# Attention lanes by head parity instead of key parity, values in one phase, and x loaded first, in a fused sliding-window attention and gated MLP kernel

## The chip, the cores and the metric

The kernel runs on one core of one Trainium2 chip. The metric is the device time of one execution in microseconds, the median of several runs. The kernel before takes 281.9 us (three runs, 280.76 to 282.53).

An execution can fall into a slower state; such runs are marked slow.

A matrix multiply on TensorE shows in the traces as two instructions, a weight load (PEld) and the matmul proper (PE): 4336 of each on the page of the kernel before. I call the two a *pair*.

## The reference, cut to what matters

```python
# x: 1 x 2048 x 512, bf16; 32 heads of 16; window 256; F = 1792
xn  = layernorm(x)
q, k, v = split(xn @ wqkv)                       # per head 2048 x 16
s   = q @ k.T * 16**-0.5
s   = where((i - j >= 0) & (i - j < 256), s, -1e9)
att = softmax(s) @ v                             # back to 2048 x 512
out = x + att @ wo + ((xn @ w_gate) * (xn @ w_up)) @ w_down
```

## The kernel before: the parts that matter

The tokens are worked off in four chunks T of 512, and in each chunk there are four groups c of eight heads, so there are 16 (T, c) pairs of attention work. A chunk has eight blocks of 64 queries. A block of queries needs five blocks of keys: its own (masked by one triangle), the one four back (masked by the other triangle) and the three between (not masked). Scores lie as keys x queries in `S`; ACT exponentiates them to `P`; POOL zeroes the triangles with selects; the values matmul then multiplies `P` by `V`, with a column of ones that gives the softmax sum.

All of this has contractions of 16 (scores) or 64 (values), so the kernel cuts TensorE's array, which a dense matmul takes as a whole (128*128 in the page's shapes), into eight tiles for it: four tiles `e`, times two *lanes* of 64 rows or columns. The rest (projections, gate, up, down, output) is 128 x 128 x 512 "dense" work. A small list scheduler in the kernel orders the work before it is issued, and drops attention blocks into the run of dense matmuls.

Before, a lane holds the key blocks of one *key parity*. V is laid out with 128 tokens on the partitions, so that key block `j` is in lane `j % 2`. A head's output needs keys of both parities, which means that both lanes add into the same PSUM place; the kernel keeps these two additions apart in time, so the values come in two phases, with a drain and a semaphore between them:

```python
def i_values(self, T, c, strips, phase, banks, begun):
    if phase == 1:
        self.nc.tensor.wait_ge(self.turn, self.v)
    # ... todo: the segments (key block k, m query blocks from q) whose head parity is lane ^ phase
    for _, lane, par, k, q, m, at, P in sorted(todo, key=lambda t: t[:2]):
        U, j = divmod(8 * T + k, 8)
        for e in range(4):
            self.nc.tensor.matmul(
                banks[par][32 * e:32 * e + 17, 64 * q:64 * (q + m)],
                lhsT=self.V[U % 3][64 * lane:64 * lane + 64, j // 2, 8 * c + 2 * e + par, 0:17],
                rhs=P[64 * lane:64 * lane + 64, e, 64 * at:64 * (at + m)],
                start=(par, e) not in begun, stop=phase == 1, tile_position=(64 * lane, 32 * e), ...)
    if phase == 0:
        self.nc.tensor.drain().then_inc(self.turn, 1)
```

The scores go out in batches (five per pair, four in chunk 0), the V projection is four plain dense matmuls per 128 tokens, and the loads and a run of useless matmuls (the *warm-up*) stand at the top:

```python
load(nc.sync,   self.x[:, 0, :], ...);  load(nc.scalar, self.Wqkv[:, :, 1024:1536], ...)   # Wv
load(nc.sync,   self.x[:, 1, :], ...);  load(nc.scalar, self.Wqkv[:, :, 512:1024], ...)    # Wk
load(nc.sync,   self.x[:, 2, :], ...);  load(nc.sync, self.x[:, 3, :], ...)
load(nc.sync,   self.Wqkv[:, :, 0:512], ...)                                               # Wq
# ... gate, up, down, output weights, the rest of x
for _ in range(40):        # the warm-up: useless matmuls
    nc.tensor.matmul(self.M[0][:, 0:128], lhsT=self.ident[:], rhs=self.ident[:], start=True, stop=True)

def matmuls(self, ps, pairs, first=True, last=True):        # all dense work
    for n, (a, b) in enumerate(pairs):
        self.nc.tensor.matmul(ps, lhsT=a, rhs=b, start=first and n == 0, stop=last and n == len(pairs) - 1)
```

The softmax here doesn't subtract the row's maximum and nothing guards it: scores larger than these inputs give would overflow.

## Time and profile before

| | kernel before |
|---|---|
| median time | 281.9 us |
| span of the profiled run | 279.4 us |
| PE busy | 96% |
| score + value matmuls | 1664 + 1664 |
| first score block | 18.15 us |

PE is the bottleneck: busy for nearly the whole span and first in the chain. The instruction queue moved 34 packets, 0.56 MB.

The timeline of the kernel before, PE only, around one pair (start us, us, engine, line, operation, count), shows an attention block between dense work: values phase one, a score batch, values phase two.

```profile
180.32 0.59 PE L218 MATMUL M<-xnT,Wg 128*128 128x512 bf16 x2
180.85 0.74 PE L255 MATMUL M<-P,V 64*17 64x64 bf16 x56
181.73 0.42 PE L226 MATMUL S<-Q,K 16*64 16x320 bf16 x16
182.09 0.77 PE L255 MATMUL M<-P,V 64*17 64x128 bf16 x56
182.79 1.04 PE L218 MATMUL M<-xnT,Wu 128*128 128x512 bf16 x4
```

I cost a block from the starts: the time from the last dense start before it to the first after it, minus one dense step (0.216 us). So costed, a score batch takes 0.45 us, and values-scores-values 2.04 us. There are no waits inside. The same view at the start of the kernel shows the first score batch at 18.15 us, and the view of the waits (waiter <- what it waited for: us in total, times, longest) shows that the layernorm statistics wait for x:

```profile
18.15 0.42 PE L226 MATMUL S<-Q,K 16*64 16x320 bf16 x16
```

```profile
DVE st L267 <- DMA x<-in_A_x_dram: 2.8, 3, 1.5
```

### The profile page before, as it was taken

How to read it: one execution, taken by the hardware profiler on the slowest of the kernel's cores; microseconds unless marked ns; L12 is line 12 of the kernel's file. 1: busy time of each engine (PE TensorE's matmuls, PEld its weight loads, DVE VectorE, ACT ScalarE, POOL GpSimd, SP SyncE). 2: the span in 40 equal slices, each digit the busy share in tenths (PEclk: the TensorE clock that was granted, in tenths of full speed). 3: DMA queues.
4: the chain of work that ended last, by engine and by line, in shares of the span. 5: the costliest groups of instructions: out<-in, count | busy, mean ns of one | idle time of the engine just before them, and what ended most of it. 6: DMA issues, size and time to landing. Idle time of an engine off the chain costs nothing.

```text
span 279.4 us, 9843 instructions
## 1 busy us (share of the span) xinstructions
PE 266.8 (96%) x4336; PEld 122.7 (44%) x4336; DVE 183.9 (66%) x323; ACT 150.8 (54%) x91; POOL 210.9 (75%) x447
## 2 busy tenths in 40 slices
PE   6699999999999999999999999999999999999994
PEld 5354444444444444444444444444444444444441
DVE  4668986879893508677884539687781518687503
ACT  2125756756575666576574756554566666564000
POOL 3208898879799999988799897879499999879000
PEclk9799999999999999999999999999999999999999
DMA  7999240000005100000005300000000000000002
GB/s 224 371 372 348 81 77 2 2 2 2 2 0 79 39 21 25 0 6 0 5 0 72 64 22 2 2 2 2 2 4 21 21 21 21 1 5 0 5 0 75
DMA packets 17050, 14.00 MB, mean 50 GB/s; under 512 B 7024, under 2 KB 17008, under 8 KB 17008
## 3 DMA queue, kind: packets, MB, share of 16 engines
q1 hardware_dynamic: 15952, 12.32, 15.6%
q10 hardware_dynamic: 1056, 1.05, 1.2%
q8 instruction: 34, 0.56, 0.9%
q14 instruction: 8, 0.07, 0.1%
HBM read 9.70 MB, written 2.10 MB: 42 GB/s over the span
## 4 chain that ended last, share of the span: by engine, by line
PE 83%; POOL 9%; DMA 2%; DVE 2%; issue 2%; ACT 1%; SPq 0%; ACTq 0%
PE M L218 68%; PE S L226 9%; POOL P L236 8%; PE M L255 6%; DMA x<-in_A_x_dram 2%; ACT P L498 1%; POOL rs L273 0%; PE M L592 0%; SPq L168 0%; DVE xnT L214 0%; DVE st L267 0%; DVE hT L688 0%; DVE gsb L214 0%; DVE V L214 0%; DVE y L709 0%
## 5 line engine op out<-in xcount | busy, mean ns | idle before, releaser
L236 POOL TENSOR_SCALAR_AFFINE_SELECT P<-P 64x256 bf16<-64x256 bf16 (+1 forms) x424 | 202.9, 501 | 40.7 <-ACT P L498 31.5
L498 ACT ACTIVATE P<-S 128x2048 bf16<-128x2048 f32 x76 | 142.6, 1877 | 86.8 <-PE S L226 77.7
L218 PE MATMUL M<-xnT,Wu 128*128 128x512 bf16 x224 | 57.7, 380 | 0.1
L218 PE MATMUL M<-xnT,Wg 128*128 128x512 bf16 x224 | 57.7, 380 | 0.0
L218 PE MATMUL M<-Wd,hT 128*128 128x512 bf16 x224 | 54.5, 380 | 0.5
L688 DVE TENSOR_TENSOR hT<-M,gsb 128x512 bf16<-128x512 f32 x56 | 37.9, 677 | 10.6 <-PE M L218 10.2
L532 DVE STREAM_TRANSPOSE at<-M 128x512 f32<-128x512 f32 x32 | 21.2, 696 | 25.7 <-PE M L255 25.5
L214 DVE CAST gsb<-M 128x512 bf16<-128x512 f32 x46 | 31.5, 686 | 7.2 <-PE M L218 6.7
L709 DVE TENSOR_TENSOR y<-M,x 128x512 bf16<-128x512 f32 x16 | 11.0, 689 | 34.7 <-PE M L218 34.6
L218 PEld LDWEIGHTS <-Wu 128*128 128x128 bf16 x224 | 20.3, 98 | 24.7 <-issue 1.3
L218 PE MATMUL M<-xnT,Wqkv 128*128 128x512 bf16 (+1 forms) x152 | 31.0, 351 | 0.0
L218 PEld LDWEIGHTS <-Wg 128*128 128x128 bf16 x224 | 20.1, 98 | 24.4 <-issue 1.2
L218 PEld LDWEIGHTS <-hT 128*128 128x128 bf16 x224 | 19.8, 98 | 24.9 <-issue 2.8
L255 PE MATMUL M<-P,V 64*17 64x192 bf16 (+4 forms) x1664 | 23.6, 240 | 0.5 <-POOL P L236 0.5
L255 PEld LDWEIGHTS <-V 64*17 64x17 bf16 x1664 | 17.4, 85 | 12.6 <-issue 8.9
L218 PEld LDWEIGHTS <-Wqkv 128*128 128x128 bf16 x152 | 13.4, 101 | 14.3 <-issue 0.9
L226 PE MATMUL S<-Q,K 16*64 16x192 bf16 (+3 forms) x832 | 17.4, 248 | 1.2
L218 PE MATMUL M<-Wqkv,xnT 128*128 128x512 bf16 x64 | 16.5, 396 | 1.6 <-DVE xnT L214 0.9
L226 PE MATMUL S<-Q,Ko 32*64 32x128 bf16 (+3 forms) x832 | 17.1, 245 | 0.1
L218 PE MATMUL M<-Wo,OT 128*128 128x512 bf16 x64 | 16.8, 380 | 0.3
L226 PEld LDWEIGHTS <-K 16*64 16x64 bf16 x832 | 7.8, 103 | 17.7 <-issue 16.5
L226 PEld LDWEIGHTS <-Ko 32*64 32x64 bf16 x832 | 8.1, 104 | 13.4 <-issue 13.4
(38 smaller groups left out, 133.1 us busy)
## 6 DMA issues: line engine op xcount, KB each, us to landing
out_dram<-y SPq DMA_DIRECT2D x16, 128.0 KB, 1.7
Wg<-in_B_w_gate_dram SPq DMA_DIRECT2D x2, 896.0 KB, 10.1
Wu<-in_B_w_up_dram SPq DMA_DIRECT2D x2, 896.0 KB, 11.5
Wd<-in_B_w_down_dram SPq DMA_DIRECT2D x1, 1792.0 KB, 17.7
Wqkv<-in_A_wqkv_dram ACTq DMA_DIRECT2D x2, 512.0 KB, 5.4
x<-in_A_x_dram SPq DMA_DIRECT2D x1, 1024.0 KB, 14.2
x<-in_A_x_dram SPq DMA_DIRECT2D x4, 128.0 KB, 5.0
Wqkv<-in_A_wqkv_dram SPq DMA_DIRECT2D x1, 512.0 KB, 6.7
```

Source lines behind the costliest of these rows:

```text
L214: self.nc.vector.tensor_copy(out=out, in_=in_)
L218: self.nc.tensor.matmul(ps, lhsT=a, rhs=b, start=first and n == 0, stop=last and n == len(pairs) - 1)
L226: self.nc.tensor.matmul(self.S[64 * lane:64 * lane + 64, e, 64 * at:64 * (at + m)], lhsT=(self.Ko if par else self.K)[U % 3][rows, c, 64 * ...
L236: self.nc.gpsimd.affine_select(out=v, in_=v, pattern=[[0, 4], [0, n], [sign, 64]], base=0, fill=0.0, compare_op=ALU.is_gt if kind else ALU ...
L255: self.nc.tensor.matmul(banks[par][32 * e:32 * e + 17, 64 * q:64 * (q + m)], lhsT=self.V[U % 3][64 * lane:64 * lane + 64, j // 2, 8 * c + ...
L498: ex = self.op(f"exp{g}", {"A": (took + 0.06, took + 0.18)}, [o], lambda e: self.nc.scalar.activation(out=P[:, :, 0:hi], in_=self.S[:, :, ...
L532: t = self.op(f"tr{v}", {"V": (0.64, 0.74)}, [o] + ts, lambda e, par=par: nc.vector.transpose(out=self.at[:, :, par, :], in_=self.M[banks[ ...
L688: x = self.op(f"u{T}.{f}", {"V": PSUM_COPY["V"]}, [o, ("gate", T, f)], lambda e: self.nc.vector.tensor_tensor(out=self.hT[T % 2][:, f, :], ...
L709: self.nc.vector.tensor_tensor(out=keep["y"][:], in0=self.M[i][:], in1=self.x[:, t, :], op=ALU.add)
```

## The change

The lanes stand for *head parity*: lane 0 holds the even heads, lane 1 the odd ones, each with every key block. The two lanes then write different banks, so the kernel does without the second phase, the drain and the semaphore. For that, it keeps each lane's V on that lane's 64 partitions, so each V projection block is computed in two 64-column tiles of the array. A batch is now the same for both lanes, and its segments are cut so that columns to be masked lie four apart, which lets one select mask two of them (64x512 for 64x256: 673 ns for 475 in the trace of the kernel before). Loads are reordered, so that x comes before the weights. In cut form (the bookkeeping of the scheduler, small changes of its cost constants, and the split of the layernorm's first step are left out):

```diff
 def layout(T):
-    # ... per lane: key blocks of that parity, in 3 or 2 groups of up to 8 query blocks
+    ends = [(0, 4, 1, 0), (1, 5, 1, 1), (4, 4, 2, 2), (2, 6, 1, 4), (3, 7, 1, 5), (4, 6, 2, 6)]   # (k, q, m, at)
+    begins = [[(0, 0, 4, 0), (1, 1, 4, 4)], [(2, 2, 4, 0), (3, 3, 4, 4)]]
+    # T = 0: begins + 2 batches; else ends, 2 batches, begins
 def i_values(...):
-        if phase == 1: self.nc.tensor.wait_ge(self.turn, self.v)
+        segments = [(P, s) for P, batch in strips for s in batch]
+        for n, (P, (k, q, m, at)) in enumerate(segments):
+            U, j = divmod(8 * T + k, 8)
+            for lane in range(2):
+                rows = slice(64 * lane, 64 * lane + 64)
+                for e in range(4):
+                    self.nc.tensor.matmul(
+                        banks[lane][32 * e:32 * e + 17, 64 * q:64 * (q + m)],
+                        lhsT=self.V[U % 3][rows, j, 4 * c + e, 0:17],
+                        rhs=P[rows, e, 64 * at:64 * (at + m)],
+                        start=n == 0, stop=n == len(segments) - 1, tile_position=(64 * lane, 32 * e), ...)
-        if phase == 0: self.nc.tensor.drain().then_inc(self.turn, 1)
 def add_v(self, T, b, land=0.0):
-            self.matmuls(self.M[i][:], [(self.xnT[..][:, k, 128 * b:128 * b + 128], self.Wqkv[:, k, 1024:1536]) for k in range(4)])
+            for jj in range(2):
+                tok = slice(128 * b + 64 * jj, 128 * b + 64 * jj + 64)
+                for k in range(4):
+                    w = self.Wqkv[:, k, 1024:1536].rearrange("p (h l d) -> p l h d", l=2, d=16)
+                    for lane in range(2):
+                        self.nc.tensor.matmul(self.M[i][64 * lane:64 * lane + 64, 256 * jj:256 * jj + 256],
+                                              lhsT=self.xnT[T % 2][:, k, tok], rhs=w[:, lane], ..., tile_position=(0, 64 * lane))
 def prologue(self):
-        # x0 | Wv ; x1 | Wk ; x2, x3, Wq
+        # x0 | x1 ; x2 | x3 ; Wv in halves on both queues ; Wk, Wq
```

Columns streamed do not change (307,200 for scores and as many for values), but 2048 + 2048 matmuls carry them instead of 1664 + 1664, and the V projection has 256 matmuls of 256 columns where it had 64 of 512.

## The prediction

> **What bounds the kernel now.** TensorE. The page shows PE busy 96% of the 279.4 us span, POOL 75%, DVE 66%, ACT 54%; the chain of waits is 83% PE and 9% POOL. The timeline shows what PE does: 512-column dense matmuls start every 0.216 us, and nearly the whole stretch from 18 us to 275 us is dense work with attention blocks put in. From starts in the timeline, minus one dense step, I cost the blocks: a score block between dense ones 0.45 us (0.21 us of streaming, the rest two changes of array tiling, about 0.12 us each); values-scores-values, 2.03 us (1.76 us in the first chunk); values phases with dense work between them, 0.98 us for the first (its drain is some 0.19 us of that) and 0.79 us for the second, and up to 0.9 us more in 75-105 us, where POOL's selects are late. Sum: 60 us of attention, against 199 us of dense steps. Before that a start: the first score block stands at 18.15 us, because x tiles come late (statistics wait 1.5 and 1.0 us for DMA) and PE idles 2.9 us and then runs at half clock.
>
> **What changes.**
> 1. Values: one phase for two; no drain and semaphore, and the scheduler nearly always issues scores, then values (15 of 16). Streaming is the same (307,200 columns); changes of tiling fall from four to three per pair. Estimate: 0.21+1.07+3x0.12 plus little = 1.7 us for the 2.03 to 2.7 us now (1.4 for 1.76 in chunk 0). All 16: minus 6 to 7 us, on the critical path.
> 2. Shorter segments: 2048 score and 2048 value matmuls for 1664 each; sixteen score blocks have 48 matmuls in six segments, many of 64 columns. In today's trace 32 matmuls cost 0.457 us against 0.450 us for 16, but a leading 64-column segment takes 52 ns rather than 27. I charge plus 1 to 2 us.
> 3. V projection in two column tiles: same streaming if the tiles overlap (8 steps of 107 ns), plus about five changes of tiling. [...] Plus 1 to 1.5 us.
> 4. Selects: 272 for 424, of which 208 (was 56) are of double width. At 673 and 475 ns: 170 us for 203. Mostly off the path; it takes away the POOL waits before values (about 1.5 us, counted in 1).
> 5. Start: x first on two queues, so all statistics run back to back; first scores at about 14 us, with about 0.4 us of dense work still owed: minus 3.5 us (2 to 5).
>
> The tail (65 dense matmuls, 14 us) is unchanged.
>
> **Sum.** -6.7 +1.4 +1.0 -3.5 = -7.8 us: **274 us**, 8 in 10 from 269.5 to 278. Faster by over 2%: 0.76; within 2%: 0.22; slower: 0.02.
>
> **What would show it.** Scores-values blocks near 1.7 us between dense steps; no drain between phases; POOL busy 165-175 us and gone from the chain; score blocks of 48 under 0.6 us; V projection blocks under 1.0 us; first scores at 13-15 us, no half-clock window; dense step still 0.216 us.
>
> **What would make it wrong.** Column tiles of V that don't overlap (up to 0.8 us x 16); 64-column weight loads that bound the short segments; values waiting for selects or banks, as a pair now needs two banks at once; weights landing later because x goes first.

Of the sum no term is cut: -6.7 +1.4 +1.0 -3.5 = -7.8 us, which gives 274. Under 3, of the charge, five changes of tiling at about 0.12 us (the estimate from the score block) make 0.6 us; that it came to 1 to 1.5 us was the author's estimate.

## More of the kernel before

The page of the kernel before gives the span, the busy time of each engine (us, share of the span, instructions), the DMA queue that the page labels "instruction" (packets, MB, share), the chain of work that ended last by engine, and groups of instructions (operation, out<-in, shapes, count | busy us, mean ns | idle before, and what ended it):

```profile
span 279.4 us, 9843 instructions
...
PE 266.8 (96%) x4336; PEld 122.7 (44%) x4336; DVE 183.9 (66%) x323; ACT 150.8 (54%) x91; POOL 210.9 (75%) x447
...
q8 instruction: 34, 0.56, 0.9%
...
PE 83%; POOL 9%; DMA 2%; DVE 2%; issue 2%; ACT 1%; SPq 0%; ACTq 0%
...
L236 POOL TENSOR_SCALAR_AFFINE_SELECT P<-P 64x256 bf16<-64x256 bf16 (+1 forms) x424 | 202.9, 501 | 40.7 <-ACT P L498 31.5
...
L255 PE MATMUL M<-P,V 64*17 64x192 bf16 (+4 forms) x1664 | 23.6, 240 | 0.5 <-POOL P L236 0.5
```

The trace has 8,700 instruction records for TensorE (4336 weight loads, as many matmuls, and a few drains and semaphore waits), which is 256 for each of the 34 packets of 16,384 bytes (255.9 by division), and the packets are spread over the run, the first at 18.3 us and the last at 265.1 us. I read this as TensorE's program being streamed in, 256 instructions at a time, while it runs.

## The result, and the profile after

The changed kernel takes **292.84 us** (median of four, 291.58 to 297.0; the 297.0 is a slow run, and the three fast ones are 291.58, 291.79 and 293.88). The ratio to the kernel before is 1.0375 (95%: 1.0304 to 1.0446): slower by 3.8%. A ratio in this document is the mean time of one kernel's fast runs over that of the other's in the same rounds, so it is not quite the ratio of the medians that are quoted. All outputs are right.

The page of the kernel after, the same lines:

```profile
span 289.8 us, 11641 instructions
...
PE 271.8 (94%) x5296; PEld 138.5 (48%) x5296; DVE 185.0 (64%) x332; ACT 153.6 (53%) x98; POOL 175.5 (61%) x289
...
q8 instruction: 41, 0.67, 1.0%
...
PE 81%; issue 7%; POOL 5%; DMA 2%; ACT 2%; SPq 1%; DVE 0%; ACTq 0%; POOLq 0%; DVEq 0%
...
L203 POOL TENSOR_SCALAR_AFFINE_SELECT P<-P 64x512 bf16<-64x512 bf16 (+1 forms) x272 | 169.0, 627 | 87.4 <-ACT P L450 75.5
...
L213 PE MATMUL M<-P,V 64*17 64x64 bf16 (+3 forms) x2048 | 26.2, 228 | 9.7 <-POOL P L203 5.3
```

The selects came out as predicted (169.0 us). But the values (L213) now stand idle for 9.7 us where they had 0.5, "issue" (time in which the engine waited for nothing that the profile shows) is 7% of the chain where it was 2%, and the instruction queue moved 41 packets for 34. The waits of the kernel after, at the values:

```profile
PEld L213 <- issue: 11.8, 9, 2.3
...
PE M L213 <- POOL P L203: 5.3, 3, 2.1
PE M L213 <- issue: 4.4, 3, 1.7
```

Read as they stand, these lines say that more than half of the idle time at the values is due to late selects. The next section shows that this reading is wrong.

In this trace the start is as predicted: the timeline of the kernel after has the first scores at 13.96 us (experiment 3 shows how much of that is luck).

```profile
13.96 0.30 PE L193 MATMUL S<-Q,K 16*64 16x256 bf16 x4
```

Three places from the timeline of the kernel after, PE only. A values block without a stall:

```profile
98.38 0.25 PE L193 MATMUL S<-Q,K 16*64 16x128 bf16 x4
...
98.74 1.58 PE L213 MATMUL M<-P,V 64*17 64x64 bf16 x136
100.26 1.04 PE L184 MATMUL M<-Wd,hT 128*128 128x512 bf16 x4
```

The same block of another pair stops two matmuls before its end, then goes on, and nothing that the profile shows had been awaited:

```profile
114.40 1.57 PE L213 MATMUL M<-P,V 64*17 64x64 bf16 x134
117.43 0.28 PE L213 MATMUL M<-P,V 64*17 64x256 bf16 x2 [1.47 <-issue]
117.64 0.60 PE L184 MATMUL M<-xnT,Wg 128*128 128x512 bf16 x2
```

And a stall in the middle of a run of plain dense matmuls, which read no selects at all:

```profile
133.90 1.25 PE L184 MATMUL M<-xnT,Wqkv 128*128 128x512 bf16 x5
136.01 0.81 PE L184 MATMUL M<-xnT,Wqkv 128*128 128x512 bf16 x3 [0.86 <-issue]
```

So I counted TensorE's instruction records one by one and looked up the index at which each stall lies. After the first scores there are seven stalls of over a microsecond, and all seven lie at an index that is 193 modulo 256; one and the same place in a block of 256, the number of records for each instruction packet (the offset of 63 to a full multiple is constant; I take it for instructions that run ahead of the first one counted, and call these places multiples of 256 from here on). Beside each I put the packet of the instruction queue that was in flight then (worked out from the records; "256 took" is the time from the first to the last start of the block before the stall, "gap" the time between the starts on both sides of the stall):

| stall begins, us | 256 took, us | fetch in flight, us | resumes, us | gap, us |
|---|---|---|---|---|
| 115.69 | 1.28 | 115.13 to 116.09 | 117.43 | 1.74 |
| 134.78 | 2.34 | 133.30 to 134.47 | 136.01 | 1.23 |
| 165.40 | 1.27 | 164.97 to 165.93 | 167.32 | 1.92 |
| 199.04 | 1.36 | 198.55 to 199.70 | 201.18 | 2.13 |
| 218.54 | 1.34 | 218.40 to 219.56 | 220.89 | 2.35 |
| 235.09 | 1.31 | 234.00 to 235.22 | 236.60 | 1.51 |
| 255.84 | 1.28 | 255.01 to 256.00 | 257.34 | 1.50 |

PE goes on 1.3 to 1.6 us after the packet has landed, every time, and 2.3 to 2.7 us after the fetch began. Three more boundaries, behind blocks of 2.7 to 3.6 us, have short stalls of some 0.25 us each (at 58.36, 86.31 and 148.88 us), and these too end 1.2 to 1.4 us after a landing. The other 30 or so pass without one. Among them is a block of only 1.68 us, whose successor's fetch had begun 3.4 us before it was needed. In the kernel before the shortest block takes 2.9 us, and there is no stall at a boundary; there the packet had landed 2.7 us ahead. So the length of a block does not decide alone: the stalls in these traces go with how long ago the next packet landed. In the eight traces that have all records (288 crossings), PE never passes a boundary sooner than 1.2 us after that landing (the shortest distance is 1.25 us in the changed kernel, at 149.15 us, and 1.56 us in the kernel before, at 247.38 us), and every stall of over 0.2 us at a boundary ends 1.2 to 1.6 us after it. The DMA view of the kernel after, window 113 to 119 us in 40 slices, shows the two packets of that stretch, the first at 115.1 us:

```profile
GB/s 0 0 0 0 0 0 0 0 0 0 0 0 0 0 109 0 0 0 0 0 0 0 0 0 0 0 0 0 0 0 0 0 0 0 0 0 0 109 0 0
...
q8 instruction: 2, 0.03, 2.3%
```

The seven gaps are 12.4 us, 12.1 us once the normal steps between starts are taken off. There is one more cost. After the longest stall of this run the array's clock fell: the view of busy time by window (window, PE busy and instructions, granted clock, DMA) has 0.50 for the 3.4 us that follow, and the trace shows a dense step of 0.426 us there for 0.216. That cost about 1.4 us, an estimate from the starts (six dense steps make 1.3 of it).

```profile
217.44 1.37 PE L213 MATMUL M<-P,V 64*17 64x64 bf16 x120
220.89 0.62 PE L213 MATMUL M<-P,V 64*17 64x256 bf16 x16 [2.08 <-POOL P L203]
```

```profile
220.80:224.20 3.40, 3.31 (x30) 0.50 0.02 5
```

This stall is also one of those that the profile puts down to a select, and it too lies at a multiple of 256.

### The profile page after: what moved, and what is told of

It reads as the page before. It is cut to its first block, busy times and chain, and to the rows that moved or that the text cites. A ratio compares the mean times of both kernels' runs of the same rounds, so it can differ in the third digit from the quotient of the medians.

```text
span 289.8 us, 11641 instructions
## 1 busy us (share of the span) xinstructions
PE 271.8 (94%) x5296; PEld 138.5 (48%) x5296; DVE 185.0 (64%) x332; ACT 153.6 (53%) x98; POOL 175.5 (61%) x289
## 4 chain that ended last, share of the span: by engine, by line
PE 81%; issue 7%; POOL 5%; DMA 2%; ACT 2%; SPq 1%; DVE 0%; ACTq 0%; POOLq 0%; DVEq 0%
PE M L184 60%; PE S L193 9%; PE M L213 7%; POOL P L203 5%; PE M L595 4%; DMA Wqkv<-in_A_wqkv_dram 2%; ACT P L450 2%; SPq L134 1%; DVE y L665 0%; DVE xnT L180 0%; DVE K L180 0%; ACTq L450 0%; POOLq L203 0%; DVEq L180 0%
## 5 line engine op out<-in xcount | busy, mean ns | idle before, releaser
L203 POOL TENSOR_SCALAR_AFFINE_SELECT P<-P 64x512 bf16<-64x512 bf16 (+1 forms) x272 | 169.0, 627 | 87.4 <-ACT P L450 75.5
L450 ACT ACTIVATE P<-S 128x2048 bf16<-128x2048 f32 x76 | 140.9, 1854 | 94.5 <-PE S L193 81.2
L644 DVE TENSOR_TENSOR hT<-M,gsb 128x512 bf16<-128x512 f32 x56 | 38.3, 683 | 12.9 <-PE M L184 12.4
L213 PE MATMUL M<-P,V 64*17 64x64 bf16 (+3 forms) x2048 | 26.2, 228 | 9.7 <-POOL P L203 5.3
L180 DVE CAST gsb<-M 128x512 bf16<-128x512 f32 x43 | 29.5, 686 | 7.4 <-PE M L184 7.4
L193 PE MATMUL S<-Q,Ko 32*64 32x64 bf16 (+3 forms) x1024 | 34.2, 234 | 0.1
L193 PE MATMUL S<-Q,K 16*64 16x64 bf16 (+3 forms) x1024 | 33.8, 234 | 0.2 <-issue 0.2
L193 PEld LDWEIGHTS <-K 16*64 16x64 bf16 x1024 | 18.3, 104 | 31.9 <-issue 31.0
L213 PEld LDWEIGHTS <-V 64*17 64x17 bf16 x2048 | 20.8, 84 | 13.3 <-issue 11.8
L193 PEld LDWEIGHTS <-Ko 32*64 32x64 bf16 x1024 | 17.7, 104 | 0.2 <-issue 0.2
L595 PE MATMUL M<-Wqkv,xnT 128*64 128x256 bf16 x256 | 15.5, 274 | 0.7 <-ACT xnT L178 0.7
## 6 DMA issues: line engine op xcount, KB each, us to landing
Wg<-in_B_w_gate_dram SPq DMA_DIRECT2D x2, 896.0 KB, 10.3
```

Source lines behind the costliest of these rows:

```text
L180: self.nc.vector.tensor_copy(out=out, in_=in_)
L193: self.nc.tensor.matmul(self.S[64 * lane:64 * lane + 64, e, 64 * at:64 * (at + m)], lhsT=(self.Ko if lane else self.K)[U % 3][rows, c, 64 ...
L203: self.nc.gpsimd.affine_select(out=v, in_=v, pattern=[[0, 4], [0, n], [sign, 64]], base=0, fill=0.0, compare_op=ALU.is_gt if kind else ALU ...
L213: self.nc.tensor.matmul(banks[lane][32 * e:32 * e + 17, 64 * q:64 * (q + m)], lhsT=self.V[U % 3][rows, j, 4 * c + e, 0:17], rhs=P[rows, e, ...
L450: ex = self.op(f"exp{g}", {"A": (took + 0.06, took + 0.18)}, [o], lambda e: self.nc.scalar.activation(out=P[:, :, 0:hi], in_=self.S[:, :, ...
L595: self.nc.tensor.matmul(self.M[i][64 * lane:64 * lane + 64, 256 * jj:256 * jj + 256], lhsT=self.xnT[T % 2][:, k, tok], rhs=w[:, lane], sta ...
```

## The experiments

Two theories for the stalls and one for the rest:

- **F, the fetch of instructions.** By the counts above (8,700 records and 34 packets of 16,384 bytes before, 10,604 and 41 after), TensorE's program arrives in blocks of 256 instructions. A packet is in flight for 1.0 to 1.2 us at the seven stalls, and PE goes on 1.3 to 1.6 us after it has landed. The theory: a block that executes in 1.3 us leaves too little time for the next one, and PE stands until it is there. The seven crossings show gaps of 1.2 to 2.4 us.
- **P, late selects** (the rival, and the profile's own wording for 5.3 us). The values now need all five strips of `P` at once, and wait for POOL.
- **R, the rate of short matmuls.** Apart from stalls, so the theory, a burst of many short matmuls is bound by how fast pairs are issued, not by the columns.

### 1. Twelve and 44 useless pairs more in the warm-up

These shift every later instruction's place in its block by 24 or 88 instructions, and change nothing else: the warm-up streams about as many columns, and no select, buffer or order of work is touched. Under P nothing should happen to the stalls. Under F they must stay at multiples of 256 and so strike other work.

```diff
-        for _ in range(40):
-            nc.tensor.matmul(self.M[0][:, 0:128], lhsT=self.ident[:], rhs=self.ident[:], ...)
+        for _ in range(52):                  # a_shift24;  a_shift88: range(84) and 0:52
+            nc.tensor.matmul(self.M[0][:, 0:96], lhsT=self.ident[:], rhs=self.ident[:, 0:96], ...)
```

> The changed kernel with 12 more warm-up weight-load/matmul pairs in front (52 of 96 columns for 40 of 128, about the same time), so every later TensorE instruction stands 24 places further on in the instruction stream; nothing else differs. Theory F (TensorE's instructions come in blocks of 256; a block of which the next is entered before it is fetched stalls the engine 1.2 to 2.4 us): block boundaries now fall 24 instructions earlier in the program, again inside the scores-values bursts: about seven stalls at 256-multiples, 12 us in all, time as the changed kernel, 289 to 295 us. Rival P (late selects on GpSimd, or banks, stop the values): no dependence on the shift, 292 us and the same stalls at the same places of the program.

> The same with 44 more pairs (84 of 52 columns), 88 places. Theory F: the boundaries then mostly miss the bursts; from the traced times of the changed kernel I work out at most 2 us of stalls in place of 12, and no half-clock window after one: 279 to 284 us. Rival P: 292 us as before.

Measured: with 24 instructions more 293.08 us, ratio to the kernel before 1.0415 (1.0388 to 1.0443). With 88 more **282.59 us**, ratio 1.0043 (1.0019 to 1.0066). Forty-four useless matmuls made the changed kernel some 9.5 us faster (profiled spans 280.3 and 289.8 us), although they delay its first scores to 16.2 us.

In the first, six stalls remain, 1.97 to 2.31 us each, 12.9 us together, and every one is again at 193 modulo 256. The block at 114.40 us above, which had stopped before its last 2 matmuls, now stops before its last 14: 12 pairs earlier, exactly the 24 instructions. This trace, too, has a window of half clock (0.50 from 205.4 to 208.9 us), after a stall of 2.21 us; the longest, of 2.31 us, has none. Timeline and waits with 24 more:

```profile
117.42 1.43 PE L213 MATMUL M<-P,V 64*17 64x64 bf16 x122
120.88 0.40 PE L213 MATMUL M<-P,V 64*17 64x256 bf16 x14 [2.04 <-issue]
```

```profile
PE M L213 <- issue: 9.3, 5, 2.0
PE M L213 <- POOL P L203: 1.9, 1, 1.9
```

In the second, most boundaries fall into slower stretches; four gaps of 0.44 to 0.76 us are left, again at multiples of 256, and there is no window of half clock after the start. Of the four dense blocks that remain (1.2 to 2.0 us), three pass without a stall: their next packet had landed 1.6 to 2.2 us ahead. The same block runs through. Timeline with 88 more, and its group of values matmuls:

```profile
116.66 1.58 PE L213 MATMUL M<-P,V 64*17 64x64 bf16 x136
118.17 1.04 PE L184 MATMUL M<-xnT,Wg 128*128 128x512 bf16 x4
```

```profile
L213 PE MATMUL M<-P,V 64*17 64x64 bf16 (+3 forms) x2048 | 24.7, 227 | 0.3 <-issue 0.3
```

The wait for selects is gone with the stalls (5.3, then 1.9, then none), with the same 272 selects. P falls; F stands. What F says is also seen to be a matter of luck: which work a boundary hits depends on the count of all instructions before it.

### 2. The values of a pair in two halves with dense work between

All parts of the change stay, and so do all 10,604 instruction records (the expectation says 10,594) and 41 packets; only the 136 matmuls go out as 72 and 64, with some dense work between, so that no 256 instructions run so densely.

```diff
     def i_values(self, T, c, strips, banks, half):
+        cut = (len(segments) + 1) // 2
         for n, (P, (k, q, m, at)) in enumerate(segments):
+            if (n >= cut) != half:
+                continue
     def choose(self):
+        if self.half is not None and self.mode != "V" and now >= self.half_end + 1.7:
+            return now, "V", None
```

> The changed kernel with the values phase of each pair cut in two halves, with about 8 dense matmuls (1.7 us) between; the same 10,594 TensorE rows. Theory F: no 256 instructions in a row are used up in under 2.5 us any more, so stalls fall to 0 to 2 us, two more changes of tiling per pair cost 15 x 0.24 = 3.6 us: 280 to 286 us. Rival P: waits for selects stay at some 5 us and the switches come on top: 293 to 297 us.

Measured: **282.28 us**, ratio to the kernel before 1.0025 (1.0000 to 1.0050), some 9 us under the changed kernel by the profiled spans (280.6 and 289.8 us). One stall is left at a boundary, of 0.4 us. The timeline:

```profile
118.11 0.82 PE L216 MATMUL M<-P,V 64*17 64x64 bf16 x72
118.86 1.04 PE L184 MATMUL M<-xnT,Wg 128*128 128x512 bf16 x4
119.74 1.03 PE L184 MATMUL M<-xnT,Wu 128*128 128x512 bf16 x4
120.69 0.98 PE L216 MATMUL M<-P,V 64*17 64x128 bf16 x64
```

The halves cost 1.21 us (with a score batch before) and 0.94 us, together 0.17 us more than the 1.97 us of the undivided block. I put that down to another two changes of array tiling, which no run isolates. This run alone would not decide between F and P, since a later half also gives the selects more time; together with the shifts it supports F. It also shows that the number of instructions is harmless here by itself (10,604 records in both, one stall of 0.4 us for seven of 1.2 to 2.4): under F, what stalls is a dense stretch that uses a block up before the next one is in.

### 3. The order of the loads alone

```diff
 # on the kernel before
-        # x0 | Wv ; x1 | Wk ; x2, x3, Wq
+        # x0 | x1 ; x2 | x3 ; Wv in halves on both queues ; Wk, Wq
-        land = (3.2, 3.6, 4.3, 4.7)
-        wv, wk, wq = 5.2, 6.6, 8.0
+        land = (3.3, 3.4, 3.9, 4.1)
+        wv, wk, wq = 5.6, 7.0, 8.4
```

> The kernel before with the change's order of loads alone (x tiles first on both queues, and the schedule's landing times with it). If the start is worth what the changed kernel's trace shows (first scores at 14 us for 18 us), it gains 2 to 4 us: 278 to 280 us, ratio 0.986 to 0.993; if the start gain is only work moved elsewhere, under 1 us.

Measured: **279.15 us**, ratio 0.9927 (0.9874 to 0.9980), a gain of about 2.1 us; the first scores stand at 15.39 us instead of 18.15.

```profile
15.39 0.42 PE L226 MATMUL S<-Q,K 16*64 16x320 bf16 x16
```

So a gain from the loads is real, at the low end of what was expected. Two things limit the reading. The trace of the kernel before has a window of half clock at the start (0.50 from 9.5 to 12.9 us) and the one of this run has none, so part of the gain may be that. And the 13.96 us of the changed kernel (with 0.4 us of dense work owed, about 3.8 us gained) is a good draw: `a_spread`, `a_merge`, `a_merge_pace` and `a_merge_pace15`, with the same loads and warm-up, have their first scores at 14.72 to 15.52 us, and three of these four show a window of half clock from 7.5 us or so that the trace of the changed kernel lacks.

### 4. Twice as many value matmuls in the kernel before

Every value matmul is cut into two of half the columns. Columns, array tiles and phases stay.

```diff
-                self.nc.tensor.matmul(banks[par][32*e:32*e+17, 64*q:64*(q+m)], ...)
+                for h in range(2):
+                    self.nc.tensor.matmul(banks[par][32*e:32*e+17, 64*q+32*m*h:64*q+32*m*(h+1)], ...)
```

> The kernel before with every value matmul cut in two of half the columns: 3,328 for 1,664, the same columns, the same schedule. Theory R: a phase of 112 matmuls takes some 1.08 us in place of 0.55, of 80 some 0.75 for 0.4: about 12 to 15 us in all; theory F adds stalls at multiples of 256 instructions, which this kernel before never had, where a values-scores-values burst (now 480 instructions) holds a boundary: 5 to 15 us more. Together 295 to 312 us. If only streamed columns count: 282 to 284 us and no stall.

Measured: 309.6 us (one round only), ratio 1.1006 (1.0961 to 1.1051). So 1664 pairs more, with not one column more, cost 28 us. Timeline of this kernel, and of the kernel before at its corresponding place:

```profile
126.73 1.18 PE L256 MATMUL M<-P,V 64*17 64x32 bf16 x112
```

```profile
117.19 0.74 PE L255 MATMUL M<-P,V 64*17 64x64 bf16 x56
```

From the first to the last start, 112 matmuls take 988 ns and 56 take 510 ns: 8.8 and 9.1 ns a pair. (In chunk 0: 80 in 738 ns, 40 in 398 ns.) A values phase costs what its *number* of pairs costs, so the kernel before was bound by the rate of pairs too, and R stands; whether the weight load or the matmul sets that rate, no run separates. Over all phases this is about 14 us (24 x 0.478 + 8 x 0.340). Most of the rest is stalls at a dozen places, the seven largest, of 1.3 to 2.0 us, making 10.8 us. They lie close to multiples of 256 records; the match is not exact here, because a few records are missing from this trace, but each of the seven ends 1.3 to 1.7 us after an instruction packet landed, as in the changed kernel. So F can be made in the kernel before, too, by nothing but more instructions.

### 5. Longer segments in the changed kernel

If many short matmuls are the trouble, the lanes by head parity can have fewer than before: with both lanes alike, a key block's query blocks can stay in one segment of up to five. That is 1440 + 1440 matmuls. The price is that masked columns no longer lie four apart, so every select masks one column (480 selects; the expectation's 512 is a miscount).

```diff
 def layout(T):
+    # T > 0
+    return [[(-1,0,4,0),(4,4,4,4)], [(-2,0,3,0),(0,0,5,3)], [(-4,0,1,0),(-3,0,2,1),(1,1,5,3)],
+            [(2,2,5,0),(5,5,3,5)], [(3,3,5,0),(6,6,2,5),(7,7,1,7)]]
 def selects(batch):
-        # two columns four apart in one select
+        out += [(kind, a, 1, 1) for a in cols]
```

> The changed kernel with each key block's queries in one segment where they were cut in two so that selects pair up: 12 segments for 17 in a pair (9 for 13 in the first chunk), 1,440 score and value matmuls each for 2,048, the same columns; all selects single, 512 for 272. Theory R (a matmul with its weight load costs TensorE about 10 ns of issue[...], so bursts of short segments are bound by their number, not by their columns): values of 96 take some 1.1 us instead of 1.3 to 1.5, no score block over 0.47 us, and a scores-values burst is under 256 instructions, so hardly a block-boundary stall: 272 to 278 us. Rival: if the segments' number is not what costs, scores-values blocks stay near 1.97 us and the time near 281 us plus waits for the slower selects. GpSimd busy 215 to 235 us may add waits of 1 to 3 us in both.

From theory R a figure of about 10 ns stands beside the 9.2 to 9.7 ns a pair of the undisturbed values bursts in the changed kernel (136 pairs from first to last start in 1238 to 1315 ns).

Measured: 286.45 us, ratio 1.0198 (1.0157 to 1.0239), so faster than the changed kernel but still slower than the one before, and outside the 272 to 278 us expected. The blocks were cheap, as R wants: values of 96 matmuls 1.37 us, score batches 0.46 us whatever their segments. Yet some 12 us went at the end, after 257 us. The scheduler's pace for score batches (one per 3.0 us) and its cost for a select (0.21 us and a term by size) were set for other batches; the last three batches and the last values had no dense work left between them (the expectations speak of five batches), so that PE waited for ACT and POOL, and the array ran at half clock for 13.7 us from 257.9 us on:

```profile
257.20 0.33 PE L189 MATMUL S<-Q,K 16*64 16x320 bf16 x4 [2.06 <-ACT P L446]
...
259.70 0.48 PE L189 MATMUL S<-Q,K 16*64 16x320 bf16 x4 [2.08 <-ACT P L446]
```

This hid the gain, so I moved the two constants.

### 6. Longer segments, with the scheduler's pace fitted

```diff
 # on the kernel of experiment 5
-    PACE = 3.0
+    PACE = 2.8
-            cost = 4 * 64 * m[2] * 0.0008 + 0.21
+            cost = 4 * 64 * m[2] * 0.0008 + 0.17      # a_merge_pace15: 0.15
```

> a_merge with the schedule told the select time that its own trace shows (model constant 0.17 for 0.21 us) and a score every 2.8 us for 3.0, so no score blocks are left for after the dense work. In a_merge PE stood or ran at half clock for some 12 us from 257 us on, because five batches were still to do; everything ahead of that ran as theory R says. If so, this takes 273 to 277 us. If the selects are what binds (512 of 0.4 us, 206 us), values wait for them all along and it stays above 280 us.

> The same with 0.15 for 0.17: values are placed closer behind their selects. 273 to 278 us; waits of values for selects show whether the margin is used up.

Measured: **272.93 us**, ratio 0.9687 (0.9662 to 0.9712), and 273.58 us, ratio 0.9742 (0.9693 to 0.9792). The first beats both kernels, the one before by 3.1%. Its page:

```profile
span 271.1 us, 9417 instructions
...
PE 262.9 (97%) x4080; PEld 129.0 (48%) x4080; DVE 187.1 (69%) x339; ACT 149.1 (55%) x91; POOL 208.0 (77%) x497
...
q8 instruction: 32, 0.52, 0.8%
...
PE 94%; DMA 3%; SPq 1%; DVE 0%; issue 0%; DVEq 0%
```

After the first scores its PE has no stall at a boundary, nor any other gap between starts over 0.4 us. POOL is as busy as in the kernel before (208 us), with the selects' count up again, and that costs nothing: it is not in the chain. So the whole of the change (lanes, one phase, column tiles of V, x first) is worth having with longer segments and a fitted pace; the segments that it cut short to spare POOL were what turned it into a loss. The pace alone was not tried, neither on the changed kernel nor on the one before, so how the gain divides between segments and pace is not shown.

## Why the prediction was wrong, point by point

Predicted 274.0 us (269.5 to 278), measured 292.84. In terms of the sum, after against before; measured terms are costed from the starts in the two traces as above, and stalls are counted by themselves:

| term | predicted, us | measured, us |
|---|---|---|
| values in one phase | -6.7 | -3.2 |
| short segments in score batches | +1.4 | +2.8 |
| V projection in column tiles | +1.0 | +1.0 |
| start | -3.5 | -3.8 |
| stalls at instruction blocks | not foreseen | +12.1 |
| half clock after one of them | not foreseen | +1.4 |
| sum | -7.8 | +10.3 (spans: +10.4) |

The three short stalls of 0.25 us are not in the table; with them the sum is some 0.7 us over the spans.

**What bounds the kernel**: right as far as it went. PE was busy for 96% of the span. But columns and changes of tiling, which the prediction counted, were not all that bound it inside the attention blocks.

**Start**: right in this trace, partly by luck. First scores were predicted at about 14 us and came at 13.96, but at 14.72 to 15.52 us in four other traces with the same loads; experiment 3 shows the order of loads alone giving 2.1 us.

**V projection**: right. The column tiles overlap: a block costs 0.91 us where four dense steps are 0.86, while its 16 matmuls of 256 columns, one after another at the dense rate, would take 1.73 us (an estimate from the step of 0.216 us).

**Selects**: right in size, 169.0 us for the predicted 170. It was also right that they are off the path: the profile's waits for them in the changed kernel vanish when 44 useless matmuls are added.

**Values**: this is the step that failed. The prediction put it as "0.21+1.07+3x0.12 plus little = 1.7 us for the 2.03 to 2.7 us now ... All 16: minus 6 to 7 us, on the critical path." Two things were wrong in it.

The greater one: it took the burst as limited by columns and tiling only, and never asked whether 336 to 368 instructions in 2 us can be supplied. The bursts before were at most 256 instructions in about 1.9 us, broken by a drain; the shortest 256 between two boundaries took 2.9 us and showed no stall. In the changed kernel a burst's 256 take 1.3 us, and at seven of some 40 boundaries PE stood for 1.2 to 2.4 us, 12.1 us together, with a window of half clock in tow. Experiments 1 and 2 show that it is the boundary, and that neither selects nor the number of instructions is the cause.

The smaller one: "plus little" was not little. An undisturbed scores-values block costs 1.97 us, not 1.7. From first to last start the 136 value matmuls take 1238 to 1315 ns, where undisturbed, and their columns need about 1080 (an estimate: eight query blocks x five key blocks x 64 columns are 2560 columns on each tile, at the dense step's 0.216 us for 512). In the middle of the burst eight 64-column matmuls take 67 to 100 ns to start, while their columns on eight tiles need 27 ns at the dense rate; only the final 256-column ones run at the columns' pace (107 ns for eight). In chunk 0 the block costs the same as before, 1.75 us. So the gain was 3.2 us.

**Short segments**: the sign was right, the size half. A score batch of 48 costs 0.63 us where one of 32 costs 0.46: 16 such, +0.175 us each. The prediction reasoned from the trace that 32 matmuls cost no more than 16. That holds, but it does not go on: the first pairs of a burst start fast (in a values burst, 16 in 63 ns) and then slow to about 9 ns each. Why the head of a burst is fast was not shown.

**What would make it wrong**: of the four that were listed, three did not come about. The second (weight loads that bound short segments) may be part of R, since a pair of 32 or of 64 columns takes some 9 ns, but no run separates the weight load from the matmul. The main cause, the fetch, was not on the list. The line of the instruction queue and the count of instructions were both on the page before.

What stays open: why PE goes on only 1.2 to 1.6 us after the packet has landed was not tested, nor what decides when a fetch begins: at the seven stalls it began 2.3 to 2.7 us before PE went on, too late for blocks of 1.3 to 2.3 us to cover it.

## What to carry to other kernels

Count instructions as well as columns: where 256 TensorE instructions (128 weight-load and matmul pairs) run in 1.3 to 2.3 us, as they did before the long stalls here, look for a stall at each multiple of 256 (blocks of about 3 us were at the edge here: some passed, some stalled for 0.2 to 0.8 us), and either spread the burst over dense work or make its matmuls longer. A stall that the profile calls "issue", or puts down to a producer that is far from saturated, is tested cheaply by adding a few useless instructions ahead of everything: if the stalls slide over the work, as they did in experiment 1, they belong to the instruction stream. When a shape is chosen to relieve an engine that has little part in the chain (here POOL, 75% busy, 9% of the chain), check what it costs in matmuls on the one that is.
